# Block-causal attention and two MLPs on one core: a planner's queue position, drains on VectorE, one more tile with seven products

## The chip, the cores and the metric

The kernel runs on one core of one Trainium2 chip. The core's engines are PE (TensorE, matrix products, with PEld for its weight loads), DVE (VectorE), ACT (ScalarE), POOL (GpSimd) and SP (SyncE, which here issues nearly all DMAs). Each engine works through its own queue in order. The metric is device time in microseconds (us) of one execution.

## The reference

Attention over q, k, v of shape (4, 8, 576, 64) under a mask by blocks of 64, then two MLPs on the 2304 tokens of width 512:

```python
    mask = block_i >= block_j
    scores = np.where(mask, scale * np.matmul(q, k.transpose(0, 1, 3, 2)), -1000000000.0)
    attn = softmax(scores)            # with 1e-09 added to the sum
    x = attn @ v                      # heads put side by side: 2304 x 512
    h = x @ w_in;  x = (h * sigmoid(h)) @ w_out             # first MLP, 512 -> 2048 -> 512
    h = x @ w_in2; g = max(h, 0) + alpha * min(h, 0)        # second MLP
    out = g @ w_out2
```

## The kernel before

**Tiles.** The 2304 tokens are nine tiles of 256. The first MLP computes in pairs of rounded parts (three products for one, `three`); one of its steps takes two of the sixteen blocks of 128 hidden columns for one tile ("lone", matmuls of 256 columns), or one block for two tiles together ("common", matmuls of 512 columns). The last two tiles, 7 and 8, share: `both(NB - 2, TOGETHER[1])` makes `TOGETHER[1]` lone steps of tile 7, then common steps, then as many lone steps of tile 8. Tile 8 holds the last 64 rows of the four sequences; its input comes back from DRAM (`load_last`) when attention has ended, so no common step can start before.

The second MLP takes tiles 0 and 1 together, step by step (eight steps each, `up2`, `act2`, `down2`), and then tiles 2 to 8 one after the other. `up2` leaves `h` in one of four PSUM banks (names h and acc). `act2` makes `u` on DVE (lines 1199 and 1203) and splits it into a high half (ACT, L325) and a low half (DVE, L1224) of `g`. `down2` has two forms. In the plain one (`n < PLAIN`, tiles 0 to 2) a step is 12 matmuls of 512 columns into two banks. In the other a step is seven products of 256 columns, three matmuls each, into four banks e, e, s, o; POOL first adds blocks of `u` (four instructions of line 1211), and `store2` puts the products together. The mixed second weights of that form, `w1om`, come from `mix_o`: a reload of `kept`, four instructions on POOL (L434), a high half on ACT and a low half on DVE (L386).

**The scale.** Each tile of the second MLP has a scale, `load2`: its activations are loaded (`xs`), DVE reduces them (L1136), the 128 partial results go out to DRAM and come back spread over all partitions (`row<-xsc`, `rows<-row`), DVE reduces again (L1146), and then the tile's input `xh` is made (ACT L325, DVE L1157).

**The drains.** `store_plain` scales a bank of 512 columns on ACT and one on DVE. `store2` starts with a copy of the first product on ACT, then has seven `scalar_tensor_tensor` on DVE (L1319) that read the four banks and add. PE may not write a bank of the next tile before these have read it.

**What sets the order.** Every operation is given to a planner (`Plan`) with an engine, a cost and a wished time `plan.at`. `Plan.order` runs a list schedule on these costs: of the operations that are ready on an engine, the one with the smallest wished time goes first. The instructions are then written out in that order, and each engine's queue keeps it. A planned cost thus never changes what is computed, only where things stand in the queues: for a DMA, `kib / 350.0` us are added to its planned landing.

```python
            dma(lambda: rows(), lambda: row().to_broadcast([128, 128]), 64, [row], [rows])
            add("DVE", dve_cost(128), lambda: nc.vector.tensor_reduce(sc()[:, 1:2], rows(), axis=AX.X, op=ALU.max),
                [rows], [sc])
```

Of the kernel before, what the change touches and what calls it, by code (L numbers as in the profile page):

```python
# [13 lines left out]
AF = mybir.ActivationFunctionType  # L14
ALU = mybir.AluOpType
# [21 lines left out]
FIRST_LOAD = (-20.0, -6.9)  # L37
EYE = -19.85
AHEAD = 4
DOWN2, STEP2, STEP_FIRST, G_PLACES = 3.0, 0.85, 1.8, 3  # L40
TOGETHER2, PLAIN, FIRST_DOWN = 2, 3, 1.8


SLACK, SPARE2, SWITCH = 0.56, 0.3, 1.0


BEHIND = 3
TOGETHER, LAST_AT = (2, 2), 56
SHARED = (8, 13)
A1 = -3.0  # L50
GAP = 1.01
# [181 lines left out]
def dve2_cost(n, pointers=0, shared=False):  # L233
    return (155 + 60 * pointers + n / 0.96) * (1.1 if shared else 1.0) * 1e-3
# [15 lines left out]
def block_causal_attention_silu_prelu(  # L250
# [14 lines left out]
    nc = tc.nc  # L265
# [3 lines left out]
    NT, DM = out.shape  # L269
# [6 lines left out]
    N2 = NT // T2  # L276
    assert (S, DM, PAIRS) == (576, 512, 4)

    plan = Plan()
    add = plan.add  # L280
# [6 lines left out]
    psum = ctx.enter_context(tc.tile_pool(name="psum", bufs=1, space=PSUM))  # L287
# [28 lines left out]
    def dma(dst, src, kib, reads=(), writes=(), after=()):  # L316
        return add("DMA", 0.5, lambda: nc.sync.dma_start(dst(), src()), reads, writes, kib / 350.0, after)
# [809 lines left out]
    def load2(n, after=()):  # L1127
        s = sb(ff2_p, [128, T2 // 32, KD, 32], F32, "xs")
        x2 = x2d[places[n]]
        for z in range(4):  # L1130
            add("DMA", 0.5, lambda z=z: nc.sync.dma_start(
                s()[32 * z:32 * z + 32].rearrange("p i k t -> p i (k t)"),
                x2()[:, 128 * z:128 * z + 128].rearrange("(i p) n -> p i n", p=32)),
                [x2], [(s, z)], extra=T2 / 350.0, after=after)
        sc = xsc[n] = sb(ff2_p, [128, 4], F32, "xsc", 3)
        add("DVE", dve_cost(KD * T2), lambda: nc.vector.tensor_reduce(  # L1136
            sc()[:, 0:1], s().rearrange("p i k t -> p (i k t)"), axis=AX.X, op=ALU.max, apply_absolute_value=True),
            [s], [sc])
        if n < TOGETHER2:
            spread(lambda: sc()[:, 0:1], [sc], lambda: sc()[:, 1:2], [sc])  # L1140
        else:
            row = sb(dram_p, [1, 128], F32, f"row{n}")
            rows = sb(ff2_p, [128, 128], F32, "rows")
            dma(lambda: row().rearrange("o p -> p o"), lambda: sc()[:, 0:1], 1, [sc], [row])
            dma(lambda: rows(), lambda: row().to_broadcast([128, 128]), 64, [row], [rows])
            add("DVE", dve_cost(128), lambda: nc.vector.tensor_reduce(sc()[:, 1:2], rows(), axis=AX.X, op=ALU.max),  # L1146
                [rows], [sc])
        m = lambda: sc()[:, 1:2].bitcast(I32)
        tiny(m, m, 0x7F800000, None, ALU.bitwise_and, None, sc)
        tiny(m, m, float(27 << 23), float(TOP << 23), ALU.max, ALU.subtract, sc)  # L1150
        add("DVE", dve_cost(6), lambda: nc.vector.reciprocal(sc()[:, 2:3], sc()[:, 1:2]), [sc], [sc])
        t = sb(ff2_p, [128, 2, KD, T2], F16, "xh2", 2)
        for kk in range(KD):
            part = lambda e, kk=kk: t()[:, e, kk].rearrange("p (i t) -> p i t", t=32)
            act(T2, lambda part=part: part(0), lambda kk=kk: s()[:, :, kk], AF.Copy, [s, sc], [(t, (0, kk))],
                scale=lambda: sc()[:, 2:3])
            add("DVE", dve_cost(T2, 1, 1), lambda part=part, kk=kk: nc.vector.scalar_tensor_tensor(  # L1157
                part(1), s()[:, :, kk], sc()[:, 2:3], part(0), op0=ALU.mult, op1=ALU.subtract),
                [s, sc, (t, (0, kk))], [(t, (1, kk))])
        for kind in "io":  # L1160
            if kind in wsc:
                add("DVE", dve_cost(1, 1, 1), lambda kind=kind: nc.vector.tensor_scalar(
                    sc()[:, 1:2], sc()[:, 1:2], wsc[kind]()[:, 2:3], 2.0**(G_EXP if kind == "i" else 0),
                    op0=ALU.mult, op1=ALU.mult), [sc, wsc[kind]], [sc])
        tiny(lambda: sc()[:, 3:4], lambda: sc()[:, 1:2], -1.0, None, ALU.mult, None, sc)
        xh2[n] = t
# [99 lines left out]
    def store_plain(n):  # L1266
        sc = xsc[n]
        e = sb(ff2_p, [128, 2, DM], F32, "osb", 2)
        for t, a in enumerate(acc.pop(n)):
            if t:  # L1270
                add("DVE", dve2_cost(DM, 1), lambda a=a: nc.vector.tensor_scalar(
                    e()[:, 1], a(), sc()[:, 1:2], None, op0=ALU.mult), [a, sc], [(e, t)])
            else:
                act(DM, lambda: e()[:, 0], lambda a=a: a(), AF.Copy, [a, sc], [(e, t)], psum=True,
                    scale=lambda: sc()[:, 1:2])
            row = 0
            for r0, count in rows_of(2 * places[n] + t):
                dma(lambda r0=r0, count=count: out[r0:r0 + count],
                    lambda row=row, count=count, t=t: e()[row:row + count, t], count * 2, [(e, t)])
                row += count  # L1280
# [18 lines left out]
    def store2(n):  # L1299
        if n < PLAIN:  # L1300
            return store_plain(n)
        sc = xsc.pop(n)
        banks = acc.pop(n)
        e = sb(ff2_p, [128, 2, DM], F32, "osb", 2)
        c11, c12, c21, c22 = ((j, half) for j in range(2) for half in range(2))
        at = lambda c: lambda: e()[:, c[0], 256 * c[1]:256 * c[1] + 256]

        def part(i):
            bank, half = SLOTS_OF[i]
            return (banks[bank], half), lambda: banks[bank]()[:, 256 * half:256 * half + 256]  # L1310

        key, m1 = part(0)
        act(256, at(c11), m1, AF.Copy, [key, sc], [(e, c11)], psum=True, scale=lambda: sc()[:, 1:2])
        for i, col, base, dst in (
            (5, 1, c11, c22), (3, 3, c22, c21), (4, 1, c22, c12), (4, 1, c21, c22), (2, 1, c11, c11), (1, 3, c21, c21),
            (6, 3, c12, c12),
        ):
            key, m = part(i)
            add("DVE", dve2_cost(256, 1), lambda m=m, col=col, base=base, dst=dst: nc.vector.scalar_tensor_tensor(  # L1319
                at(dst)(), m(), sc()[:, col:col + 1], at(base)(), op0=ALU.mult, op1=ALU.add),  # L1320
                [key, sc, (e, base)], [(e, dst)])
            for j in range(2):
                if i != {0: 6, 1: 1}[j]:
                    continue
                row = 0
                for r0, count in rows_of(2 * places[n] + 1 - j):
                    dma(lambda r0=r0, count=count: out[r0:r0 + count],
                        lambda row=row, count=count, j=j: e()[row:row + count, j], count * 2,
                        [(e, c) for c in ((c11, c12), (c21, c22))[j]])
                    row += count  # L1330
# [3 lines left out]
    for k, j in enumerate(jobs):  # L1334
        start = START[k] if k < len(START) else 2.0 * (k - PAIRS) - LEAD
        for t, f in j.steps():
            at = start + t
# [108 lines left out]
    for s in range(half + 1):  # L1446
        base = total + 1 + STEP_FIRST * s
        if s < half:
            for m in order2[2 * s:2 * s + 2]:
                plan.at = base - 1.0  # L1450
                load_w(1, "o", m, scanned)
                plan.at = base
                split_w(1, "o", m)
            for n in range(TOGETHER2):
                plan.at = base + 0.4 * n
                up2(n, s)
                act2(n, s)
            if s == 3:
                load2(TOGETHER2, after=stores[-2:])
        elif low_parts:  # L1460
            low_parts.pop()(())
        if s:
            for n in range(TOGETHER2):
                plan.at = base + FIRST_DOWN + 0.4 * n
                down2(n, s - 1)
    for n in range(TOGETHER2):
        store2(n)
    for k in range((N2 - TOGETHER2) * half + 1):
        n, s = divmod(k, half)
        n += TOGETHER2  # L1470
        base = after_first + STEP2 * k
        if n < N2:
            plan.at = base
            up2(n, s)
            act2(n, s)
            if n == TOGETHER2:
                plan.at = base + 1.0
                mix_o(s)
            if s == 1 and n + 1 < N2:
                load2(n + 1)  # L1480
        elif low_parts:
            low_parts.pop()(())
        if k >= 1:
            pn, s = divmod(k - 1, half)
            plan.at = base + DOWN2 + (SWITCH - 0.4 * s if s < 3 else 0.0)
            down2(pn + TOGETHER2, s)
            if s == half - 1:
                store2(pn + TOGETHER2)

    with tc.manual_schedule():  # L1490
# [86 lines left out]
```

## Time and profile before

| what | value |
| --- | --- |
| median of 3 runs | 913.66 us (913.22 to 916.06) |
| the profiled execution's own time | 913.75 us |
| its span in the profile | 912.0 us |
| PE busy | 885.8 us, 97% of the span |
| DVE busy | 694.3 us, 76% |
| ACT busy | 465.2 us, 51% |
| POOL busy | 263.5 us, 29% |
| mean granted PE clock | 0.996 |

The first MLP and attention take the span up to about 529 us, tiles 0 and 1 of the second MLP to about 626 us, tiles 2 to 8 the rest. The granted clock is 1.00 at 2.4 GHz.

### The profile page before, as it was taken

The page shows a single profiled execution, that of the slowest core. Times are in us where ns is not written, and L with a number is a line of the kernel's source. Part 1 is how long each engine was busy: PE and PEld are TensorE (multiplying, and loading weights), DVE is VectorE, ACT ScalarE, POOL GpSimd, SP SyncE. Part 2 cuts the span into 40 slices and gives each one's busy share as a digit, 9 for nine tenths or more (in the row PEclk, how much of TensorE's full clock was granted, in tenths as well). Part 3 has the DMA queues.
Part 4 walks back from the last instruction along what each step waited for, and adds up shares of the span by engine and source line. Part 5 has one row for each costly group of instructions (what it writes and reads, how often), then busy time and mean ns, then how long its engine had stood idle before and what let it go on. Part 6 is the DMA issues. An engine that isn't in the chain of part 4 may idle for free. (4 is left out here: it accounts for less than half of the span.)

```text
span 912.0 us, 18221 instructions
## 1 busy us (share of the span) xinstructions
PE 885.8 (97%) x6845; PEld 741.3 (81%) x6845; DVE 694.3 (76%) x1557; ACT 465.2 (51%) x1070; POOL 263.5 (29%) x380
## 2 busy tenths in 40 slices
PE   7899999999999999999999999999989999999997
PEld 5688888898988888889788786667658888888886
DVE  5999767688888888887489897896575856757673
ACT  6987556677868777775236753342122222213121
POOL 6501002232212222221000000572044544536552
PEclk9999999999999999999999999999999999999999
DMA  9952134487665766659698981441110110100010
GB/s 316 407 215 53 35 94 110 110 145 151 123 162 119 155 134 130 151 134 251 222 327 321 268 282 42 142 160 47 27 50 4 47 28 24 28 28 1 24 24 24
DMA packets 134248, 116.55 MB, mean 128 GB/s; under 512 B 100240, under 2 KB 111504, under 8 KB 134160
## 3 DMA queue, kind: packets, MB, share of 16 engines
q1 hardware_dynamic: 133008, 111.19, 44.4%
q0 software_dynamic: 1152, 4.19, 1.1%
q8 instruction: 54, 0.88, 0.5%
q14 instruction: 34, 0.28, 0.1%
HBM read 78.65 MB, written 14.16 MB: 102 GB/s over the span
## 5 line engine op out<-in xcount | busy, mean ns | idle before, releaser
L1030 PE MATMUL h<-x_all,w0i 128*128 128x256 f32 (+1 forms) x1440 | 224.7, 308 | 2.4 <-ACT x_all L325 1.5
L1030 PEld LDWEIGHTS h<-x_all,w0i 128*128 128x128 f32 x1440 | 199.8, 191 | 22.9 <-issue 3.8
L1030 PEld LDWEIGHTS <-w1i 128*128 128x128 f16 x1728 | 168.9, 98 | 24.7 <-issue 0.5
L325 ACT ACTIVATE g<-u 128x896 f16<-128x896 f32 (+1 forms) x72 | 60.7, 843 | 223.6 <-POOL u L1211 112.0
L1030 PEld LDWEIGHTS <-g 128*128 128x128 f16 x1296 | 127.2, 98 | 51.9 <-issue 8.5
L1030 PE MATMUL acc<-w0o,g 128*128 128x512 f32 x672 | 168.8, 394 | 0.2
L1211 POOL TENSOR_TENSOR u<-u 128x128 f32<-128x128 f32 x192 | 116.6, 628 | 162.9 <-DVE u L1203 75.6
L1030 PEld LDWEIGHTS acc<-w0o,g 128*128 128x128 f32 x672 | 122.4, 188 | 27.5 <-issue 2.5
L1030 PE MATMUL acc<-xh,w1i 128*128 128x256 f16 x864 | 100.0, 273 | 0.0
L335 POOL TENSOR_TENSOR g<-t,g 128x512 fp32r<-128x512 f32 x40 | 53.0, 1326 | 161.7 <-ACT g L325 157.7
L1030 PE MATMUL h<-xh,w1i 128*128 128x256 f16 x864 | 99.4, 273 | 0.0
L1224 DVE SCALAR_TENSOR_TENSOR g<-u,g 128x896 f16<-128x896 f32 (+1 forms) x72 | 74.1, 1030 | 12.7 <-ACT g L325 12.6
L325 ACT ACTIVATE p<-p,stat 128x512 f16<-128x512 f32 (+2 forms) x112 | 63.3, 608 | 22.0 <-issue 7.7
L1030 PE MATMUL e<-w1op,g 128*128 128x512 f16 (+1 forms) x336 | 67.6, 333 | 3.9 <-ACT osb L325 2.6
L325 ACT ACTIVATE p<-e,stat 128x256 f32<-128x256 f32 (+2 forms) x98 | 51.0, 527 | 33.2 <-DVE stat L946 22.3
L325 ACT ACTIVATE t<-h 128x512 f32<-128x512 f32 x72 | 43.0, 597 | 44.4 <-PE h L1030 37.7
L1030 PE MATMUL e<-w1om,g 128*128 128x256 f16 x432 | 56.6, 275 | 4.8 <-DVE osb L1319 4.2
L1075 DVE SCALAR_TENSOR_TENSOR t<-t,h 128x512 f32<-128x512 f32 x72 | 49.0, 680 | 13.7 <-ACT t L325 12.5
L325 ACT ACTIVATE g<-t 128x512 fp32r<-128x512 f32 x72 | 45.4, 630 | 19.5 <-DVE t L1075 19.0
L885 DVE SCALAR_TENSOR_TENSOR p<-p,stat,p 128x384 f16<-128x384 f32 (+1 forms) x64 | 48.4, 796 | 4.4 <-ACT p L325 4.1
L1030 PE MATMUL e<-w0o,g 128*128 128x512 f32 x192 | 49.4, 393 | 0.0
L416 POOL DMA_DIRECT2D kept<-wso x8 | 4.8, 602 | 136.2 <-DVE wso L371 70.3
(167 smaller groups left out, 1336.1 us busy)
## 6 DMA issues: line engine op xcount, KB each, us to landing
st<-qkv_b SPq DMA_DIRECT2D x16, 800.0 KB, 4.8
raw0i<-w_in SPq DMA_DIRECT2D x16, 512.0 KB, 9.9
raw0o<-w_out SPq DMA_DIRECT2D x16, 512.0 KB, 9.9
scano<-w_out SPq DMA_DIRECT2D x16, 512.0 KB, 6.6
raw1i<-w_in SPq DMA_DIRECT2D x16, 512.0 KB, 5.3
raw1o<-w_out SPq DMA_DIRECT2D x16, 512.0 KB, 5.9
scani<-w_in SPq DMA_DIRECT2D x13, 512.0 KB, 4.4
x<-x2e SPq DMA_DIRECT2D x18, 256.0 KB, 2.4
```

What stands on the lines that cost most here:

```text
L325: nc.scalar.activation(dst(), src(), func, **k)
L335: eng.tensor_tensor(lo(), src(), hi().bitcast(F32), op=ALU.subtract)
L416: add("POOL", 1.5, lambda: nc.gpsimd.dma_start(kept[s](), both().rearrange("p c n -> p (c n)")), [a, b], [kept[s]])
L885: add("DVE", dve_cost(n, 1, 1), lambda hl=hl, rr=rr, pr=pr: nc.vector.scalar_tensor_tensor(hl()[:, :, 1], pr(), rr(), hl()[:, :, 0], op0=A ...
L1030: nc.tensor.matmul(dst, lhs(a), rhs(b), start=(start and n == 0), stop=(stop and n == 2))
L1075: add("DVE", dve_cost(2 * T1), lambda: nc.vector.scalar_tensor_tensor(t(), t(), 1.0, h3(), op0=ALU.add, op1=ALU.mult), [t, h], [t])
L1211: add("POOL", pool2_cost(128, 2.5), lambda out_=out_, x=x, y=y, op=op: nc.gpsimd.tensor_tensor(u()[:, out_], u()[:, x], u()[:, y], op=op), ...
L1224: add("DVE", dve2_cost(blocks * 128, 0, True), lambda: nc.vector.scalar_tensor_tensor(side(1)(), src(), 2.0**-G_EXP, side(0)(), op0=ALU.mu ...
```

## The change

Nothing of what is computed changes but the way in which tile 2's second product is made. (1) The planned size of the `rows` DMA is 2600 instead of 64, so the planner lets it land 7.2 us later. (2) `PLAIN` is 2: tile 2 takes the seven products too, and its POOL additions with them. (3) `mix_o` is called in a loop of its own, with wished times of 6 before the steps of tile 2 instead of 1 behind. (4) All drains are on DVE: the first product's copy in `store2`, and the bank that ACT had in `store_plain`. (5) Stores have wished times 8 (tiles 0 and 1) and 5 earlier. (6) `load2(n + 1)` is called a step earlier. (7) `TOGETHER[1]` is 3: three lone steps of tile 7, ten common steps, three lone steps of tile 8; before two, twelve and two.

```diff
-DOWN2, STEP2, STEP_FIRST, G_PLACES = 3.0, 0.85, 1.8, 3
-TOGETHER2, PLAIN, FIRST_DOWN = 2, 3, 1.8
+DOWN2, STEP2, STEP_FIRST, G_PLACES, MIX = 3.0, 0.85, 1.8, 3, 6.0
+TOGETHER2, PLAIN, FIRST_DOWN = 2, 2, 1.8
...
-TOGETHER, LAST_AT = (2, 2), 56
+TOGETHER, LAST_AT = (2, 3), 56
...
-            dma(lambda: rows(), lambda: row().to_broadcast([128, 128]), 64, [row], [rows])
+            dma(lambda: rows(), lambda: row().to_broadcast([128, 128]), 2600, [row], [rows])
...
         for t, a in enumerate(acc.pop(n)):
-            if t:
-                add("DVE", dve2_cost(DM, 1), lambda a=a: nc.vector.tensor_scalar(
-                    e()[:, 1], a(), sc()[:, 1:2], None, op0=ALU.mult), [a, sc], [(e, t)])
-            else:
-                act(DM, lambda: e()[:, 0], lambda a=a: a(), AF.Copy, [a, sc], [(e, t)], psum=True,
-                    scale=lambda: sc()[:, 1:2])
+            add("DVE", dve2_cost(DM, 1), lambda a=a, t=t: nc.vector.tensor_scalar(
+                e()[:, t], a(), sc()[:, 1:2], None, op0=ALU.mult), [a, sc], [(e, t)])
...
-        act(256, at(c11), m1, AF.Copy, [key, sc], [(e, c11)], psum=True, scale=lambda: sc()[:, 1:2])
+        add("DVE", dve2_cost(256, 1), lambda: nc.vector.tensor_scalar(
+            at(c11)(), m1(), sc()[:, 1:2], None, op0=ALU.mult), [key, sc], [(e, c11)])
...
+    plan.at -= 8.0
     for n in range(TOGETHER2):
         store2(n)
+    for s in range(half):
+        plan.at = after_first + STEP2 * s - MIX
+        mix_o(s)
...
-            if n == TOGETHER2:
-                plan.at = base + 1.0
-                mix_o(s)
-            if s == 1 and n + 1 < N2:
+            if s == 0 and n + 1 < N2:
                 load2(n + 1)
...
             if s == half - 1:
+                plan.at -= 5.0
                 store2(pn + TOGETHER2)
```

**Where the instructions go, first place.** DVE's queue at the change from tile 4 to tile 5 of the second MLP; osb is the output that a store puts together, u and g are those of the next tile's steps. Before:

```order
L1224 SCALAR_TENSOR_TENSOR g_9663<-u,g_9663 128x896
L1199 TENSOR_SCALAR u<-acc,alpha_sb 128x256 x2
L1203 SCALAR_TENSOR_TENSOR u<-acc,u 128x512
L1319 SCALAR_TENSOR_TENSOR osb<-e,xsc,osb 128x256
L1224 SCALAR_TENSOR_TENSOR g_9720<-u,g_9720 128x896
L1319 SCALAR_TENSOR_TENSOR osb<-e,xsc,osb 128x256 x2
L1319 SCALAR_TENSOR_TENSOR osb<-s,xsc,osb 128x256
L1319 SCALAR_TENSOR_TENSOR osb<-e,xsc,osb 128x256
L1319 SCALAR_TENSOR_TENSOR osb<-o,xsc,osb 128x256
L1319 SCALAR_TENSOR_TENSOR osb<-s,xsc,osb 128x256
```

The same place of the change:

```order
L1224 SCALAR_TENSOR_TENSOR g_9799<-u,g_9799 128x896
L1199 TENSOR_SCALAR u<-acc,alpha_sb 128x256
L1309 TENSOR_SCALAR osb<-e,xsc 128x256
L1199 TENSOR_SCALAR u<-acc,alpha_sb 128x256
L1316 SCALAR_TENSOR_TENSOR osb<-e,xsc,osb 128x256
L1203 SCALAR_TENSOR_TENSOR u<-acc,u 128x512
L1316 SCALAR_TENSOR_TENSOR osb<-e,xsc,osb 128x256 x2
L1316 SCALAR_TENSOR_TENSOR osb<-s,xsc,osb 128x256
L1316 SCALAR_TENSOR_TENSOR osb<-e,xsc,osb 128x256
L1316 SCALAR_TENSOR_TENSOR osb<-o,xsc,osb 128x256
L1316 SCALAR_TENSOR_TENSOR osb<-s,xsc,osb 128x256
L1224 SCALAR_TENSOR_TENSOR g_9856<-u,g_9856 128x896
```

The first copy (L1309) is now in DVE's queue, and all seven additions stand ahead of the low half g of step 2 instead of around it.

**Second place.** DVE's queue between the two reductions of a scale (L1136 and L1146), in the first steps of tile 5. Before:

```order
L1136 TENSOR_REDUCE xsc<-xs 128x1
L1203 SCALAR_TENSOR_TENSOR u<-h,u 128x512
L1224 SCALAR_TENSOR_TENSOR g_9784<-u,g_9784 128x896
L1199 TENSOR_SCALAR u<-h,alpha_sb 128x256 x2
L1203 SCALAR_TENSOR_TENSOR u<-h,u 128x512
L1224 SCALAR_TENSOR_TENSOR g_9881<-u,g_9881 128x896
L1146 TENSOR_REDUCE xsc<-rows 128x1
```

The same place of the change:

```order
L1136 TENSOR_REDUCE xsc<-xs 128x1
L1199 TENSOR_SCALAR u<-h,alpha_sb 128x256 x2
L1203 SCALAR_TENSOR_TENSOR u<-h,u 128x512
L1224 SCALAR_TENSOR_TENSOR g_9931<-u,g_9931 128x896
L1199 TENSOR_SCALAR u<-h,alpha_sb 128x256 x2
L1203 SCALAR_TENSOR_TENSOR u<-h,u 128x512
L1224 SCALAR_TENSOR_TENSOR g_10023<-u,g_10023 128x896
L1199 TENSOR_SCALAR u<-acc,alpha_sb 128x256 x2
L1203 SCALAR_TENSOR_TENSOR u<-acc,u 128x512
L1224 SCALAR_TENSOR_TENSOR g_10063<-u,g_10063 128x896
L1199 TENSOR_SCALAR u<-acc,alpha_sb 128x256 x2
L1146 TENSOR_REDUCE xsc<-rows 128x1
```

The second reduction, which needs the DMAs, stands almost two steps of PE's work later: the u of steps 6 and 7 come ahead of it.

**Third place.** PE's queue where the first MLP goes over to tiles 7 and 8 together; h are up products, e and acc down products, w0i and w0o the weights. One piece of the difference:

```order
 L1030 MATMUL e<-w0o_413,g 128x512 x6
 L1030 MATMUL e<-w0o_492,g 128x512 x6
-L1030 MATMUL h<-x_all,w0i_652 128x512 x12
-L1030 MATMUL h<-x_all,w0i_700 128x512 x6
+L1030 MATMUL h<-x_all,w0i_652 128x256 x12
+L1030 MATMUL h<-x_all,w0i_700 128x256 x12
+L1030 MATMUL h<-x_all,w0i_729 128x512 x9
 L1030 MATMUL e<-w0o_603,g 128x512 x6
 L1030 MATMUL e<-w0o_616,g 128x512 x6
```

The 512-column products (the first that need tile 8) come 24 matmuls of 256 columns later.

## Rows read from the trace of the kernel before

**Rows 1.** The page: busy us (share of the span) and instructions of each engine.

```profile
PE 885.8 (97%) x6845; PEld 741.3 (81%) x6845; DVE 694.3 (76%) x1557; ACT 465.2 (51%) x1070; POOL 263.5 (29%) x380
```

**Rows 2.** PE's waits from 430 us on: us in total, times, longest.

```profile
PE e L1030 <- DVE osb L1319: 4.2, 4, 1.5
PE e L1030 <- ACT osb L325: 2.6, 1, 2.6
PE h L1030 <- ACT x_all L325: 1.5, 1, 1.5
PE e L1030 <- DVE g L1224: 1.3, 1, 1.3
```

**Rows 3.** Stretches: PE, PEld, DVE, ACT, POOL busy; granted clock, DMA share, GB/s.

```profile
450.00:455.00 5.00, 3.99 (x9) 2.97 (x10) 2.67 (x4) 2.38 (x4) 0.00 (x0) 0.66 0.94 336
680.00:685.00 5.00, 4.46 (x30) 3.26 (x28) 4.76 (x7) 0.95 (x1) 2.96 (x5) 0.66 0.29 105
535.00:560.00 25.00, 25.00 (x191) 18.73 (x190) 24.85 (x47) 9.81 (x15) 1.07 (x2) 1.00 0.48 161
575.00:625.00 50.00, 50.00 (x347) 33.71 (x346) 44.23 (x68) 20.05 (x28) 34.75 (x35) 1.00 0.37 125
```

**Rows 4.** PE's timeline, first MLP: start, us, instructions, [idle before <-releaser].

```profile
451.52 5.71 PE L1030 MATMUL h<-x_all,w0i 128*128 128x512 f32 x17 [0.23 <-DVE x_all L335]
...
469.31 2.88 PE L1030 MATMUL h<-x_all,w0i 128*128 128x512 f32 x12
...
520.57 3.04 PE L1030 MATMUL h<-x_all,w0i 128*128 128x256 f32 x24
```

**Rows 5.** Timeline where the second MLP begins: a low half g, the first down product.

```profile
544.05 0.68 DVE L1224 SCALAR_TENSOR_TENSOR g<-u,g 128x512 f16<-128x512 f32 x1
...
546.06 2.75 PE L1030 MATMUL e<-w1op,g 128*128 128x512 f16 x12
```

**Rows 6.** PE's timeline, tile 2 and the change to tile 3.

```profile
633.67 2.75 PE L1030 MATMUL e<-w1op,g 128*128 128x512 f16 x12
...
679.63 0.49 PE L1030 MATMUL e<-w1op,g 128*128 128x256 f16 x3 [2.64 <-ACT osb L325]
...
683.94 2.78 PE L1030 MATMUL acc<-xh,w1i 128*128 128x256 f16 x24
```

**Rows 7.** POOL's timeline: its first additions for the seven products.

```profile
668.27 2.60 POOL L1211 TENSOR_TENSOR u<-u 128x128 f32<-128x128 f32 x4 [47.69 <-ACT xh L325]
```

**Rows 8.** The chain that ended last: start, us, what; a scale's DMAs, the last tile change.

```profile
682.41 7.70 DMA row<-xsc
690.17 4.71 DMA rows<-row
...
878.44 5.24 PE h L1030 x48
883.68 1.31 PE e L1030 x12
```

**Rows 9.** DVE's waits from 560 us on: us in total, times, longest.

```profile
DVE xsc L1146 <- DMA rows<-row: 54.4, 7, 9.9
```

**Rows 10.** Timeline of all engines at the change from tile 4 to tile 5.

```profile
758.48 0.95 ACT L325 ACTIVATE g<-u 128x896 f16<-128x896 f32 x1 [3.12 <-DVE u L1203]
...
759.34 0.46 ACT L325 ACTIVATE osb<-e,xsc 128x256 f32<-128x256 f32 x1
...
760.23 1.17 DVE L1224 SCALAR_TENSOR_TENSOR g<-u,g 128x896 f16<-128x896 f32 x1
...
760.84 0.49 PE L1030 MATMUL e<-w1op,g 128*128 128x256 f16 x3
...
762.50 0.47 DVE L1319 SCALAR_TENSOR_TENSOR osb<-e,xsc,osb 128x256 f32<-128x256 f32 x1
...
763.02 0.81 PE L1030 MATMUL e<-w1om,g 128*128 128x256 f16 x6 [1.36 <-DVE osb L1319]
```

**Rows 11.** DVE's low halves g with 896 columns, 690 us to the end.

```profile
L1224 DVE SCALAR_TENSOR_TENSOR g<-u,g 128x896 f16<-128x896 f32 x44 | 51.8, 1178 | 11.6 <-ACT g L325 11.6
```

## The prediction

> **What bounds the kernel now.** I read the page's busy times first: PE is busy 97% of the span, the next engine 76% [rows 1]. A gain can thus only come from fewer matmuls, from PE's few waits, or from stretches in which its clock is low. So the waits of PE came second. From 430 us on there are four entries that matter, 4.2, 2.6, 1.5 and 1.3 us [rows 2]; that is 9.6 us. Third I read the clock by stretches: it is 1.00 (2.4 GHz) nearly everywhere, but 0.66 at 450 to 455 and at 680 to 685 [rows 3], each time right behind a stall of PE. There PE is "busy" at half speed for a while, which no list of waits shows. The timelines came last, to price each place.
>
> All sums are made against the profiled execution's 913.75 us, which is 0.09 above the median of the runs.
>
> **A. Entry of tiles 7 and 8 in the first MLP (part 7).** PE waits 1.5 us for `x_all` of tile 8 on ACT [rows 2] and 0.23 more on DVE; the 17 matmuls behind it take 5.71 us [rows 4]. Twelve of the same shape take 2.88 later [rows 4], so 17 would be 2.88 x 17/12 = 4.08, and 1.6 us go to the clock. The order's third place puts 24 more matmuls of 256 columns ahead of the first 512-column product: 3.04 us [rows 4]. Tile 8's input is late by only 1.5 + 0.23 = 1.7, and its loads and transposes stand where they stood, so I let the wait and the half clock go. The two added lone steps (one for each tile) have the same columns as the two common ones that they replace, in twice the instructions: 3.04 against 2.88 each, 2 x 0.16 = 0.3. Gain 1.5 + 1.6 - 0.3 = **2.8**.
>
> **B. Tile 2 with seven products (part 2).** A plain step is 12 matmuls of 512 columns, which is 24 of 256; a step with seven products is 21 of 256. Twelve of 256 take 1.31 us [rows 8], 0.109 each. Gain 8 steps x 3 x 0.109 = **2.6**. What it adds lies on other engines: 32 additions on POOL at 2.60 us for four [rows 7], eight times, on an engine that is idle 71% of the span; wider parts of `g` on ACT and DVE (896 columns instead of 512: 1178 ns [rows 11] against 0.68 [rows 5], so 0.5 x 8 = 4 us of DVE over the tile's 8 steps); seven additions instead of one scaling at its end. None of it is on the path while PE's step lasts 4.9 us: 21 x 0.109 = 2.29 for the products and 2.62 for 24 up matmuls, half of 48 in 5.24 [rows 8].
>
> **C. The scale (parts 1 and 6).** DVE waits 54.4 us in seven waits for `rows`, up to 9.9 each [rows 9]; the DMAs take 7.70 and 4.71, 12.4 together [rows 8]. What hurts is what stands behind the reduction in DVE's queue. Before, two low halves and two `u` separate the reductions (order, second place), some 4 us of DVE, less than the 12.4 by more than 8; after, `u` of four steps and three low halves, which PE's pace spreads over almost two steps of 4.9 us more, an estimated 13 us from L1136. That covers 12.4 us, so the reduction finds its rows. Most of the 54.4 costs nothing, since `u` and `g` run ahead of PE. Only PE's 1.3 us on DVE's `g` [rows 2] come from it. Gain **1.3**. The scale comes later, but the tile needs it only when its input is made, more than a step behind.
>
> **D. Change from tile 2 to tile 3 (parts 2, 3, 4 and 6).** PE waits 2.64 us on ACT's drain of tile 2 [rows 2, 6]. From 679.63 to 683.94 PE then needs 4.31 us for a step's seven products [rows 6], against 21 x 0.109 = 2.29: 2.0 more, a second short wait and the half clock of that stretch [rows 3]. In the change this place is a tile change like the later ones, with the mixed weights made and the seven products ahead and behind. Gain 2.6 + 2.0 = **4.6**.
>
> **E. The four later tile changes (parts 4 and 5).** Here PE waits 4.2 us in total on L1319 [rows 2]. The timeline of 4 to 5 shows why: ACT makes a `g` (758.48) before it copies the first product (759.34), so DVE's additions start late; then a low half of 1.17 us stands between them (760.23); PE, which needs the banks, stands 1.36 us until 763.02 [rows 10]. After the change (order, first place) the copy is DVE's own and stands right behind a `u`; all seven additions come ahead of the next low half. The fifth addition, the last to read the bank that PE wants, ended at about 763.0 when PE went on. Without the low half ahead (1.17) and without ACT's `g` ahead of the copy (0.95) it ends near 760.9; PE wanted that bank at 763.02 - 1.36 = 761.66 [rows 10]. It just fits, by 0.8. The low half that was pushed behind the drains ends near 763, and PE asks for it only after the rest of this step's products and 24 up matmuls, at least 4 us after 761.66. As a control, at the last change, where no scale and no following step crowd DVE, the products start at 883.68 without a gap behind 878.44 + 5.24 [rows 8]. Gain **4.2**.
>
> **Edits costed at nothing.** The two 512-column drains moved from ACT to DVE belong to tiles 0 and 1, whose banks wait for nobody for several us; if that cover were gone they would cost two scalings, under 1.5 us. The mixed weights (part 3) are the same instructions and reloads, earlier; they take their time on POOL and on SP's queue beside tiles 0 and 1 (first rival). The stores' DMAs go out earlier and nobody waits for them until the end, which is unchanged.
>
> **What comes back.** Sum of the gains: 2.8 + 2.6 + 1.3 + 4.6 + 4.2 = 15.5. The margins that are left are thin: 0.8 us at E's banks, and at the start of the second MLP 1.3 us between the end of the first low half, 544.05 + 0.68 = 544.73, and PE's first down product at 546.06 [rows 5], with DVE full there (24.85 of 25 us [rows 3]). PE now arrives 2.8 us earlier and DVE may not. Bounds of this: nothing, or all of A's 2.8 given back. I take 1.0, nearer to nothing, since ACT (9.81 of 25) can make up time. Forecast: 913.75 - 15.5 + 1.0 = **899.3 us**. Its own range is 897 to 902.
>
> **A rule that speaks against the change.** Low halves `g` of 896 columns take 1178 ns on the mean [rows 11],. In the Trainium skill, page "SBUF — State Buffer", section "SBUF: two separate sides", a DVE instruction with two SBUF inputs and a GpSimd one that reads SBUF share a port pair as an exclusive lock, for a whole instruction. By that rule DVE's halves and POOL's additions of tile 2 would block one another, and so would the mixes moved beside tiles 0 and 1. The rows agree in so far as a low half with 1.75 times the columns takes 1178 against 680 ns, 1.73 times, in tiles where POOL adds: at most little is lost there. By the page the sum would lose what the last rival loses, without it nothing.
>
> **Rivals.**
>
> *First: tile 2's start is crowded.* The eight mixes come first on POOL, then the additions for tile 2. Before, POOL's first additions came at 668.27, 47.69 us after its work before, so the mixes ended at 620.6 [rows 7]. With 2.60 for four additions, and about as much for ACT and DVE to split the sums, `g` of tile 2's first step is ready near 625.5; PE asks for it at 633.67 [rows 6], now 2.8 earlier, 630.9. The slack is 5.4 us. For it: all eight reloads of `kept` must pass SP's queue beside the loads of tile 2 and the scale's DMAs, and the last mix now competes with POOL's 34.75 of 50 busy us [rows 3]. Against it: the slack is more than two mixes. At 8 us late PE waits 2.6, and loses 1.5 to the clock as in A: 899.3 + 4.1 = **903.4**. Chance 0.14.
>
> *Second: A is given back.* The three lone steps keep weights of three blocks until tile 8's lone steps use them, and DVE is full at the start of the second MLP [rows 3]. Then PE waits at the first down products for what it won before, 2.8 and half of a clock loss: 899.3 + 3 to 4 = **903**. For it: 1.3 us of margin [rows 5]. Against it: ACT has room. Chance 0.14.
>
> *Third: the change does not do what it says.* The planner's 2600 stand only in its books. If the DMAs take longer than 12.4 us at the new place, DVE still waits, PE's stalls C and E stay: 899.3 + 1.3 + 4.2 = **904.8**; with a low clock behind each of them 907. Chance 0.05.
>
> *Fourth, on the other side: DVE becomes the bound of tiles 0 and 1.* There, from 575 to 625, DVE is busy 44.23 of 50 us and POOL 34.75 [rows 3], so DVE has 5.8 us to spare per 50. All the mixes now lie beside these eight double steps. If DVE's instructions lengthen beside POOL's, PE starts to wait when they grow by more than 13%. To lose what is won (14.5) and 2.7 more, DVE must grow by 5.8 x 2 + 17.2 = 28.8 us over the 97 us of the two tiles, a third. That gives **916.4**. For it: a margin of only 5.8 in 50, and the mixes' own low halves on DVE. Against it: the mixes were mostly beside these steps before (they ended at 620.6) and PE never waited there. Chance 0.05.
>
> **How the numbers follow.** Forecast 0.62, the rivals 0.14, 0.14, 0.05 and 0.05. About 0.3% of this kernel's time, 2.7 us, is what can be told from no change: faster means below 910.9, slower above 916.4. The first three rivals are still faster. Half of the fourth is no measurable change; to slower I add mishaps that I do not see, 0.07 in all; same 0.05, faster 0.88. The range goes from 896.5 (nothing comes back, and some of the clock's loss elsewhere goes) to 905, which takes in the first three rivals' times, without the low clock that the third may add.
>
> **What would show it right or wrong.** PE's waits from 430 us on lose the entries on ACT `osb`, ACT `x_all` and DVE `g`, and those on L1319 (now L1316) fall below 1 us. The clock is 1.00 at 450 to 455 and at the change from tile 2 to tile 3. DVE's waits for `rows` fall from 54.4 to under 10. PE is busy some 5 us less: 2.6 of products and 3 of clock. I am wrong if a new wait appears at tile 2's first down products (first rival), at 540 to 550 (second), if `rows` still ends DVE's waits (third), or if PE waits for DVE's `u` or `g` between 545 and 625 (fourth).

## The result, and the profile after

The change takes 898.43 us (median of 4 runs, 897.74 to 898.74) beside 913.44 us for the kernel before in the same measurement (912.96 to 916.06). The ratio is 0.983, with a 95% interval of 0.981 to 0.985. The forecast was 899.3 us with a range of 896.5 to 905. The profiled execution took 898.74 us with a span of 897.0, 15.0 less than the span before.

The page's busy times of the change, which answer to [rows 1]:

```profile
PE 879.4 (98%) x6941; PEld 749.4 (84%) x6941; DVE 706.7 (79%) x1572; ACT 464.0 (52%) x1061; POOL 281.9 (31%) x412
```

PE is busy 6.4 us less (some 5 were predicted), so some 8.6 of the 15.0 us were idle time. PE's waits of the change from 430 us on, which answer to [rows 2] (us in total, times, longest):

```profile
PE h L1030 <- DVE t L1075: 1.3, 1, 1.3
PE o L449 <- ACT ar L325: 1.1, 1, 1.1
PE acc L1030 <- POOL g L335: 0.6, 1, 0.6
PE h L1030 <- DVE x_all L998: 0.2, 1, 0.2
```

All four entries of [rows 2] are gone; every wait that is left lies in the first MLP, and the largest is new. DVE's waits for `rows` from 560 us on, 54.4 us in seven before [rows 9]:

```profile
DVE xsc L1146 <- DMA rows<-row: 0.7, 1, 0.7
```

The clock of the stretch that stood at 0.66 before [rows 3] is 1.00 in the change, as it is at the change from tile 2 to tile 3 (PE, PEld, DVE, ACT, POOL busy; granted clock, DMA share, GB/s):

```profile
450.00:455.00 5.00, 3.69 (x29) 3.37 (x28) 1.99 (x4) 2.38 (x5) 0.00 (x0) 1.00 0.86 280
```

PE's timeline of the change, with the same points as [rows 6] (start, us, instructions): the 48 up matmuls ahead of tile 2's products, the 48 ahead of tile 3's, and the next up matmuls.

```profile
627.45 5.40 PE L1030 MATMUL h<-xh,w1i 128*128 128x256 f16 x48
...
666.75 5.40 PE L1030 MATMUL h<-xh,w1i 128*128 128x256 f16 x48
...
674.28 2.78 PE L1030 MATMUL acc<-xh,w1i 128*128 128x256 f16 x24
```

From such points the gain divides without any list of waits. Before, the first block started at 628.43 and the second at 671.58, and the third row stood at 683.94:

```profile
628.43 5.40 PE L1030 MATMUL h<-xh,w1i 128*128 128x256 f16 x48
...
671.58 5.40 PE L1030 MATMUL h<-xh,w1i 128*128 128x256 f16 x48
```

| stretch | predicted | measured |
| --- | --- | --- |
| up to the 48 up matmuls ahead of tile 2 (A) | 2.8 | 628.43 - 627.45 = 0.98 |
| tile 2's products (B and C) | 2.6 + 1.3 | 43.15 - 39.30 = 3.85 |
| change from tile 2 to 3 (D) | 4.6 | 12.36 - 7.53 = 4.83 |
| the four later changes (E) | 4.2 | 8.13 + 9.18 + 8.88 + 9.31 - 4 x 7.53 = 5.38 |
| given back | -1.0 | 0 |
| sum | 14.5 | 15.0 |

A tile change is measured here from the 48 up matmuls to the next 24; without a stall it takes 7.53 us. E is larger than predicted because the waits of [rows 2] are each 0.29 us shorter than the time lost. The list counts from the modelled end of the last matmul; that lies 0.16 us behind the point where the next would have started. The other 0.13 are the six matmuls behind the wait, which take 0.78 us from start to start (763.80 - 763.02) instead of 0.66.

At the entry of tiles 7 and 8 the change's timeline shows the new wait:

```profile
450.30 3.03 PE L1030 MATMUL h<-x_all,w0i 128*128 128x256 f32 x24
451.19 0.63 ACT L325 ACTIVATE x_all<-xl 128x512 fp32r<-128x512 f32 x1 [4.94 <-DMA xl<-x_last]
452.64 0.63 ACT L325 ACTIVATE x_all<-xl 128x512 fp32r<-128x512 f32 x1 [0.81 <-DMA xl<-x_last]
453.17 0.58 ACT L325 ACTIVATE t<-h 128x512 f32<-128x512 f32 x1
...
453.91 0.68 DVE L1075 SCALAR_TENSOR_TENSOR t<-t,h 128x512 f32<-128x512 f32 x1
454.64 1.66 PE L1030 MATMUL h<-x_all,w0i 128*128 128x512 f32 x6 [1.31 <-DVE t L1075]
```

The reloaded input `xl` of tile 8 shares a ring of two places with the `t` of the lone steps, and it stands ahead of them on ACT. The `t` of a lone step whose products were done near 447.5 is made at 453.17, right behind the second `x_all`, and PE waits for the bank that it frees. The matmuls that the order's third place puts ahead did cover the wait for `x_all`; the prediction did not ask what else uses the places in which the input lands.

### The profile page after: what moved, and what is told of

The parts are those of the page before. It is cut to its first block, busy times and chain, and to the rows that moved or that the text cites. A ratio compares the mean times of both kernels' runs of the same rounds, so it can differ in the third digit from the quotient of the medians.

```text
span 897.0 us, 18472 instructions
## 1 busy us (share of the span) xinstructions
PE 879.4 (98%) x6941; PEld 749.4 (84%) x6941; DVE 706.7 (79%) x1572; ACT 464.0 (52%) x1061; POOL 281.9 (31%) x412
## 4 chain that ended last, share of the span: by engine, by line
PE 62%; DMA 3%; DVE 2%; ACT 1%; issue 1%; POOL 0%; DVEq 0%; SPq 0%; ACTq 0%
PE h L1030 20%; PE acc L1030 18%; PE e L1030 12%; PE s L1030 5%; PE o L1030 3%; DMA scani<-w_in 2%; PE e L734 2%; PE o L908 1%; DMA raw1i<-w_in 1%; PE s L734 1%; PE o L918 0%; ACT p L325 0%; DVE stat L852 0%; DMA xl<-x_last 0%; DVE t L1075 0%
## 5 line engine op out<-in xcount | busy, mean ns | idle before, releaser
L1211 POOL TENSOR_TENSOR u<-u 128x128 f32<-128x128 f32 x224 | 136.0, 627 | 125.6 <-DVE u L1203 105.7
L325 ACT ACTIVATE g<-u 128x896 f16<-128x896 f32 (+1 forms) x72 | 63.2, 878 | 215.1 <-POOL u L1211 138.8
L1030 PEld LDWEIGHTS <-g 128*128 128x128 f16 x1368 | 133.9, 98 | 32.7
L1224 DVE SCALAR_TENSOR_TENSOR g<-u,g 128x896 f16<-128x896 f32 (+1 forms) x72 | 76.4, 1062 | 10.6 <-ACT g L325 10.6
L1199 DVE TENSOR_SCALAR u<-acc,alpha_sb 128x256 f32<-128x256 f32 x72 | 32.2, 478 | 46.3 <-PE acc L1030 45.0
L1030 PE MATMUL e<-w1om,g 128*128 128x256 f16 x504 | 64.2, 273 | 0.0
L1030 PE MATMUL e<-w1op,g 128*128 128x256 f16 (+1 forms) x264 | 49.5, 311 | 0.0
```

What stands on the lines that cost most here:

```text
L325: nc.scalar.activation(dst(), src(), func, **k)
L1030: nc.tensor.matmul(dst, lhs(a), rhs(b), start=(start and n == 0), stop=(stop and n == 2))
L1199: add("DVE", dve2_cost(T2, 1), lambda c=c, m=m: nc.vector.tensor_scalar(u()[:, 2 * c:2 * c + 2].rearrange("p i t -> p (i t)"), h()[:, T2 * ...
L1211: add("POOL", pool2_cost(128, 2.5), lambda out_=out_, x=x, y=y, op=op: nc.gpsimd.tensor_tensor(u()[:, out_], u()[:, x], u()[:, y], op=op), ...
L1224: add("DVE", dve2_cost(blocks * 128, 0, True), lambda: nc.vector.scalar_tensor_tensor(side(1)(), src(), 2.0**-G_EXP, side(0)(), op0=ALU.mu ...
```

## The experiments

The time of before differs between chips: 913.4 us on the first, 908.2, 912.2 and 912.7 on those of the three groups below. A time is compared within its group; a stretch of a trace is compared directly. On the chip with 908.2 no trace of before was kept, so how large its stalls were there is not known; the expectations of the first group were worked out from the trace on the first chip.

### Scale or drains: which part removes the stalls?

**The kernel before with the longer planned scale alone.**

```diff
-            dma(lambda: rows(), lambda: row().to_broadcast([128, 128]), 64, [row], [rows])
+            dma(lambda: rows(), lambda: row().to_broadcast([128, 128]), 2600, [row], [rows])
```

> The kernel before with the planned size of the rows DMA at 2600 and nothing else changed. Theory 1 (as predicted: the order of the drains makes the stalls at the tile changes, the scale only PE's one wait on g): only term C goes, about 1.2 us, so 912.2 us; the stretch from the 48 up matmuls to the next 24 at the four later tile changes stays at 8.1 to 9.3 us. Theory 2 (DVE comes to every tile change late, from the wait for rows in the middle of the tile, and the drains are late for that): the four changes fall to about 7.5 us (5.4 us in all), and much of the 4.8 us at the change from tile 2 to tile 3 goes too: 902 to 905 us.

Measured: 902.65 us against 908.21, ratio 0.994 (0.993 to 0.996). The tile changes, the one from tile 2 to 3 among them, take 7.54 us each, and the products of tile 2 41.67 instead of 43.15. PE has no wait left in the second MLP. Theory 2 holds: with this one number alone, the stalls of terms C, D and E are absent. Against the trace of before they are 1.5 + 4.8 + 5.4 = 11.7 us, while the gain within the group is 5.6; how the 5.6 divide on this chip, where before itself is faster, is not shown. The change from tile 4 to 5 of this kernel, with the drains in their old order, beside [rows 10] and the row of before that dates it:

```profile
755.60 5.40 PE L1030 MATMUL h<-xh,w1i 128*128 128x256 f16 x48
```

```profile
747.67 0.47 ACT L325 ACTIVATE osb<-e,xsc 128x256 f32<-128x256 f32 x1 [0.31 <-PE e L1030]
...
748.53 0.47 DVE L1319 SCALAR_TENSOR_TENSOR osb<-e,xsc,osb 128x256 f32<-128x256 f32 x1
748.92 1.24 DVE L1224 SCALAR_TENSOR_TENSOR g<-u,g 128x896 f16<-128x896 f32 x1
749.10 5.40 PE L1030 MATMUL h<-xh,w1i 128*128 128x256 f16 x48
750.09 0.86 DVE L1319 SCALAR_TENSOR_TENSOR osb<-e,xsc,osb 128x256 f32<-128x256 f32 x2
```

The low half still stands between the additions, and the copy is still ACT's. But the copy now waits for PE and starts 1.4 us ahead of the 48 up matmuls at 749.10; before it started 3.7 us behind theirs (759.34 against 755.60). DVE and ACT were late as a whole.

**The kernel before with the drains alone**: the first copy on DVE, stores wished 5 earlier.

```diff
-        act(256, at(c11), m1, AF.Copy, [key, sc], [(e, c11)], psum=True, scale=lambda: sc()[:, 1:2])
+        add("DVE", dve2_cost(256, 1), lambda: nc.vector.tensor_scalar(
+            at(c11)(), m1(), sc()[:, 1:2], None, op0=ALU.mult), [key, sc], [(e, c11)])
...
+                plan.at -= 5.0
                 store2(pn + TOGETHER2)
```

> The kernel before with the first product's copy of the seven on DVE and its stores wished 5 earlier; the rows DMA stays at 64, tile 2 plain. Theory 1: the four later tile changes lose their stalls, 5.4 us, so 908.0 us, with DVE's waits for rows still near 54 us. Theory 2: DVE is late as before and gets the copy on top; at most half of the 5.4 us goes, 910.5 to 913.5 us.

Measured: 904.55 us against 908.21, ratio 0.996 (0.995 to 0.998). The kept execution (902.43) is the second fastest of twelve. In it the four later changes take 7.53 or 7.54 us too, although DVE waits 54.2 us for `rows`; the change from tile 2 to 3, whose drain this edit leaves as it was, takes 10.05 and still shows waits on `osb`. For E theory 1 holds as well: either edit is enough by itself.

DVE had not caught up at the first of these changes. Its `u` at 708.67 comes 0.98 us ahead of the 48 up matmuls, as late as before, where the same `u` came between 0.38 and 1.57 us ahead and the changes took 8.13 to 9.31. So the order itself removes the stall there. Behind it DVE gains: the first reduction of the next scale comes 6.3 us behind the 48 up matmuls (715.99 - 709.65) instead of 7.8 (723.51 - 715.71), and at the next two changes `u` is 2.44 and 3.20 us ahead.

```profile
708.67 0.69 DVE L1203 SCALAR_TENSOR_TENSOR u<-acc,u 128x512 f32<-128x512 f32 x1
...
709.65 5.40 PE L1030 MATMUL h<-xh,w1i 128*128 128x256 f16 x48
...
715.99 1.21 DVE L1136 TENSOR_REDUCE xsc<-xs 128x1 f32<-128x1024 f32 x1
728.56 0.28 DVE L1146 TENSOR_REDUCE xsc<-rows 128x1 f32<-128x128 f32 x1 [7.14 <-DMA rows<-row]
```

**The change with the planned scale back at 64.**

```diff
-            dma(lambda: rows(), lambda: row().to_broadcast([128, 128]), 2600, [row], [rows])
+            dma(lambda: rows(), lambda: row().to_broadcast([128, 128]), 64, [row], [rows])
```

> The changed kernel with the planned size of the rows DMA back at 64. Theory 1: DVE waits some 50 us for rows again, PE loses only term C: 899.6 us. Theory 2: the tile changes, now with the drains in front, are late again by a part of what they were, and the change from tile 2 to tile 3 too: 902 to 907 us.

Measured: 908.78 us against 908.21 for before, ratio 1.001 (0.999 to 1.002). The whole gain is gone. The four later changes stay at 7.53, so the loss is elsewhere: tile 2, now with the seven products, takes 47.31 us instead of 39.30, and the change behind it 9.65. PE's three largest waits of this kernel from 430 us on:

```profile
PE e L1030 <- DVE g L1224: 4.1, 1, 4.1
PE e L1030 <- DVE xsc L454: 1.9, 1, 1.9
PE e L1030 <- DVE osb L1316: 1.7, 2, 1.1
```

and its clock in the stretch right behind the first (PE, PEld, DVE, ACT, POOL busy; granted clock, DMA share, GB/s):

```profile
645.00:650.00 5.00, 5.00 (x37) 3.99 (x36) 4.78 (x11) 1.09 (x2) 2.81 (x5) 0.76 0.39 108
```

Both theories are short of the size. The first of these waits follows from `rows` directly: DVE sits idle 6.19 us for it until 641.10, makes the low half `g` at 642.35, and PE goes on at 643.59.

```profile
641.10 0.28 DVE L1146 TENSOR_REDUCE xsc<-rows 128x1 f32<-128x128 f32 x1 [6.19 <-DMA rows<-row]
...
643.59 0.28 PE L1030 MATMUL e<-w1op,g 128*128 128x256 f16 x1 [4.08 <-DVE g L1224]
```

Why tile 2 suffers most was not tried; it has two waits for `rows` in it (642.26 and 665.46 in the trace of before), and with the seven products PE asks for its `g` sooner.

This kernel also gives the clearest pair for E. Before, at the change from tile 6 to 7, and in this kernel, at the change from tile 3 to 4, DVE is equally late up to the first copy: `u` is 0.38 and 0.41 us ahead of the 48 up matmuls. From there only the order differs. Before:

```profile
836.82 0.69 DVE L1203 SCALAR_TENSOR_TENSOR u<-acc,u 128x512 f32<-128x512 f32 x1
837.20 5.40 PE L1030 MATMUL h<-xh,w1i 128*128 128x256 f16 x48
...
841.57 0.49 DVE L1319 SCALAR_TENSOR_TENSOR osb<-e,xsc,osb 128x256 f32<-128x256 f32 x1 [1.36 <-ACT osb L325]
...
844.23 0.47 DVE L1319 SCALAR_TENSOR_TENSOR osb<-e,xsc,osb 128x256 f32<-128x256 f32 x1
...
844.75 0.81 PE L1030 MATMUL e<-w1om,g 128*128 128x256 f16 x6 [1.49 <-DVE osb L1319]
```

The change with the scale at 64:

```profile
715.04 0.69 DVE L1203 SCALAR_TENSOR_TENSOR u<-acc,u 128x512 f32<-128x512 f32 x1
...
715.45 5.40 PE L1030 MATMUL h<-xh,w1i 128*128 128x256 f16 x48
...
718.02 0.47 DVE L1316 SCALAR_TENSOR_TENSOR osb<-e,xsc,osb 128x256 f32<-128x256 f32 x1
...
720.19 0.47 DVE L1316 SCALAR_TENSOR_TENSOR osb<-e,xsc,osb 128x256 f32<-128x256 f32 x1
...
721.02 1.15 PE L1030 MATMUL e<-w1om,g 128*128 128x256 f16 x9
```

The fifth addition, which PE needs, ends 7.50 us behind the start of the 48 up matmuls before (844.70 - 837.20) and 5.21 here (720.66 - 715.45). The first change takes 9.31 us, the second 7.53.

**The change with copy and stores as before, 2600 kept.**

```diff
-        add("DVE", dve2_cost(256, 1), lambda: nc.vector.tensor_scalar(
-            at(c11)(), m1(), sc()[:, 1:2], None, op0=ALU.mult), [key, sc], [(e, c11)])
+        act(256, at(c11), m1, AF.Copy, [key, sc], [(e, c11)], psum=True, scale=lambda: sc()[:, 1:2])
...
-                plan.at -= 5.0
```

> The changed kernel with the first product's copy back on ACT and the stores of tiles 2 to 8 at their old wished times, so that an addition, a low half and six additions follow each other on DVE as before; 2600 stays. Theory 1: the stalls of the tile changes come back, 5.4 us for four and one more at tile 2: 904 to 905 us. Theory 2: DVE is in time, the order does not matter: within 0.6 us of 898.4, the changes at 7.5 us.

Measured: 897.5 us against 908.21, ratio 0.988 (0.987 to 0.990). The later changes take 7.53, PE waits on no drain. Theory 2 holds: with the scale planned longer, moving the copy and the stores is worth nothing.

### The spread of the kernel before

**Both kernels again on another chip.**

> The kernel before, unchanged, on the chip of the four earlier runs, where its median was 908.2 us against 913.4 us on the first chip. Theory 1 (its stalls are a matter of when the scale's DMAs land, which differs between chips): the trace shows the four later tile changes at under 8.1 us each instead of 8.1 to 9.3, or no low clock behind the entry of tiles 7 and 8, and some 5 us less in these places together. Theory 2 (the chip is faster throughout): the stretches without stalls are shorter too, the 48 up matmuls under 5.2 us.

> The changed kernel on this chip. Theory 1: it has no stalls that depend on the landing, so its time is that of the first chip, 897.5 to 898.5 us, and the gain over before is 10 us here instead of 15. Theory 2: it is 5 us faster too, 893.5 us.

Measured: 912.87 us (910.3 to 913.8) and 900.2 us (896.9 to 902.1); before beside them 912.22, ratios 1.001 (0.999 to 1.003) and 0.987 (0.984 to 0.989). The group did not run on the chip with 908.2, so what made before faster there stays open; the change's median is above both of its expected times. The second theory is out for the two chips seen: 48 up matmuls take 5.24 in both traces. What the trace of before (910.3 us) does show is that its stalls vary: the four later changes take 7.53, 8.28, 8.49 and 8.21 us, 2.4 above the stall-free time instead of 5.4. And its entry of tiles 7 and 8 has the same wait, without the low clock of [rows 3, 4]:

```profile
450.00:455.00 5.00, 3.73 (x14) 2.58 (x15) 2.34 (x4) 2.47 (x5) 0.00 (x0) 1.00 0.83 284
```

```profile
451.03 0.50 PE L1030 MATMUL h<-x_all,w0i 128*128 128x512 f32 x1 [1.49 <-ACT x_all L325]
451.76 4.45 PE L1030 MATMUL h<-x_all,w0i 128*128 128x512 f32 x17 [0.23 <-DVE x_all L335]
```

17 matmuls take 4.45 us here and took 5.71 there. The clock's loss in term A belonged to one execution, and by this pair it was 1.26 us, not 1.6.

### The three lone steps

**The kernel before with three lone steps**, and later **the change with two**.

```diff
-TOGETHER, LAST_AT = (2, 2), 56
+TOGETHER, LAST_AT = (2, 3), 56
```

> The kernel before with three lone steps of tiles 7 and 8 (ten common ones) and nothing else. Theory 1 (as predicted: the wait for tile 8's input and the low clock go, the lone steps cost 0.3): 2.8 us below before if before shows the low clock, 1.2 if it does not. Theory 2 (tile 8's input sits in the two places of the ring t that the lone steps need, and PE waits 1.3 us for t instead of 1.5 for the input): 0 to 1 us below before, PE's waits from 430 us on show t of line 1075 with 1.2 to 1.6 us, and no low clock behind it.

> The changed kernel with two lone steps of tiles 7 and 8 as before. Theory 1 (term A as predicted): 2.8 us above the change. Theory 2 (three lone steps only change the wait on tile 8's input into one on t): within 1.2 us of the change, with a wait of about 1 to 1.5 us on x_all; 2 to 3 us above only if its profile shows the low clock behind that wait.

Measured: before with three steps 912.7 us against 912.22, ratio 1.001 (0.999 to 1.002). The change with two steps took 898.37 us beside 899.11 for the change in the same group; their ratios to before are 0.985 (0.983 to 0.988) and 0.985 (0.983 to 0.987). Theory 2 holds from both sides: where one waits for `x_all` (1.3 us), the other waits for `t` (1.2 us).

**The change with tile 8's input reloaded one step later.**

```diff
-TOGETHER, LAST_AT = (2, 3), 56
+TOGETHER, LAST_AT = (2, 3), 57
```

> The changed kernel with the reload of tile 8's input one step later in the program, so that it comes behind the second lone step's t in the ring of two places. Theory 1 (the ring makes PE's new wait): the 1.3 us on t of line 1075 go, 896.5 to 897.5 us where the change has 898. Theory 2 (the input itself is the limit): PE waits for x_all instead, about as long, and the time stays within 0.5 us of the change.

Measured: 897.14 us (896.4 to 899.1) beside 900.2 for the change (896.9 to 902.1), ratio to before 0.984 (0.982 to 0.986). The wait on `t` is gone and none on the reloaded `x_all` came, so the ring made it. The profiled execution has 3.1 us on DVE's earlier `x_all` of line 998 instead, a wait that was between 0 and 3.1 us in the traces of these kernels.

### Tile 2, and the better version

**The change again, and with tile 2 plain.**

```diff
-TOGETHER2, PLAIN, FIRST_DOWN = 2, 2, 1.8
+TOGETHER2, PLAIN, FIRST_DOWN = 2, 3, 1.8
```

> The changed kernel again, as the measure for the three that run with it. If its spread of 897 to 902 us comes from the stretch before 465 us of the span, where DVE's x_all of line 998 and the wait on t of line 1075 came out between 0.2 and 3.1 us in the runs so far, its second MLP is the same to 0.1 us as in its other traces: 7.53 us at every tile change.

> The changed kernel with tile 2 plain, as before, all else as changed. Theory 1 (term B is 8 steps of three matmuls fewer, 0.33 us each): 2.6 us above the change run beside it, the change from tile 2 to tile 3 without a stall. Theory 2 (the seven products on both sides are also what makes that change smooth, term D): a wait on osb there and 4 to 7 us above the change.

Measured: 899.11 us (897.4 to 900.3) and 901.04 us (900.0 to 902.4), ratios to before 0.985 and 0.987 (0.985 to 0.989). The seven products are worth 1.9 us by the medians and 41.68 - 39.30 = 2.38 in the traces. Theory 1 holds: the change from tile 2 to 3 takes 7.54 with tile 2 plain too. The change's own second MLP is the same to 0.01 us as in its other traces.

**The change with copy and stores as before and the later reload.** 
```diff
-TOGETHER, LAST_AT = (2, 3), 56
+TOGETHER, LAST_AT = (2, 3), 57
...
-        add("DVE", dve2_cost(256, 1), lambda: nc.vector.tensor_scalar(
-            at(c11)(), m1(), sc()[:, 1:2], None, op0=ALU.mult), [key, sc], [(e, c11)])
+        act(256, at(c11), m1, AF.Copy, [key, sc], [(e, c11)], psum=True, scale=lambda: sc()[:, 1:2])
...
-                plan.at -= 5.0
```

> The changed kernel with the first copy back on ACT and the old wished times of the stores, and with tile 8's input reloaded one step later. Theory 1 (with the scale planned longer the drains' part of the change is not needed, and the later reload takes PE's wait on t away): 0.3 to 1.5 us below the change, tile changes at 7.53 us, no wait on t of line 1075. Theory 2 (the drains on DVE matter): 1 to 5 us above the change, with waits on osb.

Measured: 895.85 us (895.3 to 897.1) beside 899.11 for the change (897.4 to 900.3), ratio to before 0.982 (0.980 to 0.984). Its median is the lowest of all. PE's only wait from 430 us on is this:

```profile
PE o L449 <- ACT ar L325: 0.7, 1, 0.7
```

Its tile changes take 7.53 or 7.54 us. The 3.3 us below the change, more than the 0.3 to 1.5 expected, are all made before the second MLP: the 48 up matmuls ahead of tile 2 start at 624.58 instead of 627.83. Some of that is the waits upstream, which vary; the 1.2 us on `t` are what the edit removes.

## Why the prediction was right, and where it was not

The time came out within 0.9 us, but not every term did: A was 1.8 us too high, E 1.2 too low, and the 1.0 that was to come back did not. That these nearly cancel is luck.

**A failed.** With "I let the wait and the half clock go" it came to 2.8 us. The wait went and a new one of 1.31 us came, on the ring shared by input and lone steps. The low clock was not a property of the place. Before with three lone steps is no faster than before, so the medians show nothing of the term; in the one pair of traces it is 0.98.

**B was right in kind**, 2.4 instead of 2.6, since 12 matmuls of 512 columns take a little less than 24 of 256. The cover held: POOL's first additions for tile 2 begin at 623.41 right behind the mixes, as the first rival had it, and ACT's first `g` of them at 626.30, 6.4 us ahead of PE's products at 632.69.

**C and D were right**, 1.5 and 4.8 for 1.3 and 4.6, but the working of D credited four parts, where the change takes 7.54 us with the scale's new size alone.

**E was right, and only half of the cause.** A stall at these changes needs two things: DVE late, and the old order of the drains. The prediction worked out the order, and there its working held: with the drains in front and DVE as late as before, the fifth addition ends 5.2 us behind the start of the 48 up matmuls, where it had 5.3 (760.9 - 755.60), and no stall is left. It did not ask why DVE was late. The bracket of its own row, `[3.12 <-DVE u L1203]` on ACT's `g` [rows 10], said that ACT had been idle for DVE; and DVE was late because of the 54.4 us in [rows 9], which the prediction called mostly free, "since u and g run ahead of PE". That lead is what the waits used up. The control that it cites, the last change without a gap, pointed there: that change has the old order too, and no scale; its copy starts at 876.84, 1.4 us ahead of the 48 up matmuls at 878.28, as in the kernel with the scale alone. So the change held two remedies, each enough, and the gain of E was credited to one.

**Nothing came back at the start of the second MLP.** PE's lead of 0.98 us was the same at its start (539.83 - 538.85, the first 48 up matmuls there) and at tile 2. **The second rival** was right that A would be lost, and wrong about where. **The third** did not come, since DVE's waits fell to 0.7 us. Its price for waits that stay was too low: in the change at 64, tile 2 and the change behind it take 47.31 + 9.65 instead of 39.30 + 7.53, 10.1 us more. **The fourth** did not come: from 575 to 625 POOL is busy 32.15 and DVE 45.52 of 50 us, against 34.75 and 44.23 [rows 3].

```profile
575.00:625.00 50.00, 50.00 (x343) 33.35 (x342) 45.52 (x67) 18.63 (x25) 32.15 (x37) 1.00 0.36 126
```

## What to carry to other kernels

A wait of an engine that is off the critical path is free only as long as its lead lasts; add up what it does between the wait and the next point where PE needs it. When a drain is late, ask two questions: what stands ahead of it in its queue, and what its engine waited for one or two steps earlier. Test each remedy alone, since two that are each enough look like one in the sum. When a load is moved or given cover, ask which other tiles share its buffers.

## What the runs showed that was not expected

A wait of about 1.5 us on PE was followed by the lower clock in one execution (17 matmuls in 5.71 us) and not in another of the same program (4.45 us), so a loss of clock read from a single trace is not a fixed cost. It came again in the change with tile 2 plain: behind a wait of 1.7 us on `ar` of line 325 the granted clock is 0.66 from 520 to 525 us, and in the trace of the change from the same group 1.00 behind a wait of 1.8. And the same program's median differed by 5 us between chips (908.2 and 913.4). In its two traces, both from slower chips than the one with 908.2, the stall-free stretches agree to 0.01 us and the stalls at the four later tile changes do not: 5.4 and 2.4 us.
